# Folded output weights, packed attention output, full units for the last heads, and an ordered start in a two-block attention kernel

## The chip, the cores and the metric

The kernel runs on one core of one Trainium2 chip. The time is the device time of one execution in microseconds, from the first to the last instruction of the core with its start and end included. A kernel is run several times and the median is quoted. The trace of one execution gives a span that is some 2 us shorter than its time. An execution counts as slow, and is kept out of comparisons, when it lies more than 1.5% above the fastest one of the same kernel.

TensorE does the matmuls, VectorE and ScalarE the elementwise work and the copies out of PSUM, GpSimd small things, SyncE starts most transfers (its queue is SPq in the profile, that of ScalarE is ACTq).

## The reference

Two attention blocks of the same size work on separate inputs: 2,048 rows, width 640, 32 heads of 20. A is softmax attention, B is linear attention with the feature map phi.

```python
def _A_ref(x, wqkv, wo):
    q, k, v = split(x @ wqkv)                      # 32 heads of 20
    p = softmax(einsum("bhqd,bhkd->bhqk", q, k) * 20 ** -0.5)
    return merge(einsum("bhqk,bhkd->bhqd", p, v)) @ wo

def _B_ref(x, wqkv, wo):
    phi = lambda t: jnp.where(t > 0, t + 1, jnp.exp(t)) + 1e-6
    pq, pk = phi(q), phi(k)
    kv  = einsum("bhsd,bhse->bhde", pk, v)
    num = einsum("bhqd,bhde->bhqe", pq, kv)
    den = einsum("bhqd,bhd->bhq", pq, pk.sum(s))[..., None] + 1e-6
    return merge(num / den) @ wo

return concatenate([A, B], axis=-1)                # inputs times 0.05, bf16
```

## The kernel before

A's scores are small, so the exponential is replaced by its polynomial of second order: products of K's 20 columns (the features, on VectorE) are multiplied with V into a table f_Tu, and the same products of Q, taken unit by unit, are multiplied with that table. A unit is 512 rows of Q by 6 heads of 20 columns, 120 partitions. 32 heads make five such units and a short one of two heads.

```python
# first loads: x in two halves and K's weights whole, then V's weights
sch.dma("act", lambda e: e.dma_start(self.w[:, 1], awq[:, :, D_MODEL:2 * D_MODEL]), writes=(("w", 1),))
xnl(0)
sch.dma("sp", lambda e: e.dma_start(self.w[:, 2], awq[:, :, 2 * D_MODEL:3 * D_MODEL]), writes=(("w", 2),))
xnl(1)
# ... Q's columns are permuted on GpSimd:
sch.op("pool", lambda e, c=c: e.tensor_copy(
    self.w[:, 0, c, 0:600].rearrange("p (b a h) -> p b a h", b=5, h=6),
    self.w0r[:, c, 0:600].rearrange("p (b h a) -> p b a h", b=5, h=6)), ...)
# ... t_psi: a unit's Q rows come back from DRAM; the short unit (c == 5) needs six loads
if c < 5:
    fns = [lambda e: e.dma_start(sl[:, 0:4, :], self.q_load(c, qc, 0, 4, 1, True)),
           lambda e: e.dma_start(sl[:, 9:11, :], self.q_load(c, qc, 7, 2, 3, True))]
else:
    for x, (d, st, nj) in enumerate(((0, 0, 3), (0, 2, 3), (6, 2, 3), (1, 2, 3), (7, 2, 2))):
        fns.append(lambda e, ...: e.dma_start(self.slot[0:40 * nj, s, x, :], self.q_load(5, qc, d, nj, st, False)))
    fns.append(lambda e: e.dma_start(self.slot[80:120, s, 4, :], self.q_load(5, qc, 0, 1, 0, False)))
# ... t_norm, t_out: A's normalised output goes to DRAM (f_Od) and comes back in another layout
self.ost[G] = self.spd(fns, (m,), (("OTw", ow),), (("Od", G),), prio=0.6)
ol = self.spd([lambda e: e.dma_start(self.OTp[:, k], self.Od.ap()[:, col].rearrange("(c p) q -> p c q", p=128))], ...)
# ... B: numerator matmuls, then each of 20 results times the reciprocal of the denominator
sch.op("dve", lambda e: e.scalar_tensor_tensor(
    oT[:, c, :], ps[:, j.bank, :], self.cn[:, c:c + 1], self.Rb[:, k, :], op0=ALU.add, op1=ALU.mult), ...)
```

Cuts are marked by "...". The program does not write instructions in a fixed order. At build time a list scheduler simulates the engines with durations written in the code, and each time an engine is free takes the ready task of the lowest priority number. 21 of those numbers are constants that were fitted for this program:

```python
_C = dict(q=1.24, qs=0.0, ks=-0.005, kd=0.02, bk=1.83, bks=-0.005, bq=6.44, bo=0.03, out=0.46, pv=0.002,
          fe=1.73, psi=5.5, r=-1.04, f=0.92, nm=2.51, op=2.71, kv=1.87, npo=2.33, bqs=0.002,
          bd=-0.79, bn=3.42)
```

The order of every engine's instructions follows from them. Memory is reused, and the profile names it by its first user: f_xT also holds A's raw output, f_wB also B's reciprocals, f_Tu first the raw Q weights, f_pk first x.

## Time and profile before

| | before |
|---|---|
| time, median of 3 runs | 359.45 us (358.58 to 362.37) |
| span of the trace | 358.7 us |
| TensorE busy; mean granted clock | 303.6 us; 0.951 |
| of that, at full clock / lost to the clock | 290.3 / 13.3 us |
| TensorE idle | 55.1 us |
| moved by DMA | 58.85 MB |

The row "at full clock" is used throughout: the busy time of TensorE in each stretch of 5 us times the clock granted in that stretch, added up. It is what the same work would take with the clock never lowered. Full-clock work, clock loss and idle time add up to the span.

The prediction shows the main views. One stretch of the chain of waits of the kernel before is added here, because it became important afterwards (columns: start in us, us, engine or transfer with tile and line). It is a short unit on its way in:

```profile
181.35 0.91 SPq L1594
182.26 0.04 issue
182.31 0.69 SPq L1594
182.99 0.04 issue
183.03 2.31 SPq L1594
185.34 0.04 issue
185.38 7.86 DMA f_big<-f_Qd
193.24 0.02 issue
193.26 1.30 DVE f_big L1607 x2
```

The reader is to see that the engine at the top is the queue of SyncE: a load of a short unit holds it for 0.7 to 2.3 us before the next can start, and the fifth of the six loads lands 7.86 us after it was started. Only then does VectorE form the products. In shares of the span, that chain is

```profile
PE 53%; DMA 15%; DVE 11%; POOL 8%; SPq 6%; issue 5%; ACT 1%; ACTq 0%; DVEq 0%
```

so starting transfers took 6% of it, and GpSimd 8%.

### The profile page before, as it was taken

What the parts mean: (1) busy time and instruction counts of PE and PEld (TensorE: products, weight loads), DVE (VectorE), ACT (ScalarE), POOL (GpSimd) and SP (SyncE); (2) the same over time, 40 slices, a digit from 0 to 9 for tenths busy, and PEclk for the clock granted to TensorE, in tenths of its full rate; (3) what the DMA queues carried; (4) which work ended last, traced back from release to release, by engine and by line L of the source; (5) the groups of instructions that cost most, each with busy time, mean ns of one, the idle gap of its engine ahead of it and who ended that gap; (6) DMA issues with size and microseconds to landing.
All of it is one profiled execution on the core that took longest, in us unless ns stands there. A gap on an engine that the chain in (4) does not pass through costs nothing.

```text
span 358.7 us, 14998 instructions
## 1 busy us (share of the span) xinstructions
PE 303.6 (85%) x6834; PEld 198.4 (55%) x6834; DVE 253.3 (71%) x350; ACT 180.1 (50%) x377; POOL 31.3 (9%) x49
## 2 busy tenths in 40 slices
PE   5989579999998899879988299982999868789955
PEld 2657347777764356546744178741554324658723
DVE  2589699999988986878896349795658767441330
ACT  2775647888884235444433235442355535335413
POOL 0049880000020100000000000000000000000000
PEclk9999989999999699998999879998799989999988
DMA  7999548214247258277736947579874466566642
GB/s 264 250 212 136 90 92 248 57 49 126 59 132 201 62 133 246 65 190 201 191 119 178 203 119 256 146 166 242 227 206 140 133 185 213 164 228 199 210 141 82
DMA packets 63571, 58.85 MB, mean 164 GB/s; under 512 B 21036, under 2 KB 59980, under 8 KB 63500
## 3 DMA queue, kind: packets, MB, share of 16 engines
q1 hardware_dynamic: 58940, 49.99, 53.9%
q10 hardware_dynamic: 4560, 7.83, 7.3%
q8 instruction: 55, 0.90, 1.2%
q14 instruction: 16, 0.13, 0.1%
HBM read 39.65 MB, written 14.48 MB: 151 GB/s over the span
## 4 chain that ended last, share of the span: by engine, by line
PE 53%; DMA 15%; DVE 11%; POOL 8%; SPq 6%; issue 5%; ACT 1%; ACTq 0%; DVEq 0%
PE ps L172 52%; DMA f_big<-f_Qd 4%; SPq L1594 4%; DMA f_w<-f_Od 4%; POOL f_w L1157 3%; POOL f_st L1248 3%; DMA f_Rc<-f_xT 2%; DMA f_dc<-f_dn 2%; DMA f_pk<-in_A_x_dram 2%; DVE f_Tu L1449 2%; DMA f_wB<-f_Bd 1%; DVE f_pk L1993 1%; DVE f_big L1607 1%; DVE f_big L1357 1%; DVE f_big L1362 1%
## 5 line engine op out<-in xcount | busy, mean ns | idle before, releaser
L1607 DVE TENSOR_TENSOR f_big<-f_big 120x1536 bf16<-120x1536 bf16 (+2 forms) x68 | 67.6, 1001 | 8.4 <-DMA f_big<-f_Qd 7.0
L172 PE MATMUL ps<-f_wB,f_xB 128*32 128x320 bf16 x1280 | 52.2, 311 | 10.1 <-issue 8.0
L172 PE MATMUL ps<-f_big,f_Tu 120*32 120x512 bf16 (+2 forms) x880 | 53.4, 384 | 3.1 <-issue 1.7
L172 PEld LDWEIGHTS ps<-f_wB,f_xB 128*32 128x32 bf16 x1280 | 37.5, 100 | 21.7 <-issue 9.6
L172 PE MATMUL ps<-f_w,f_xT 128*32 128x320 bf16 x1280 | 48.4, 307 | 0.4 <-issue 0.2
L172 PEld LDWEIGHTS ps<-f_w,f_xT 128*32 128x32 bf16 x1280 | 34.3, 100 | 11.3 <-issue 0.8
L172 PEld LDWEIGHTS ps<-f_big,f_Tu 120*32 120x32 bf16 (+2 forms) x880 | 27.7, 98 | 23.2 <-issue 3.1
L1092 ACT COPY f_xT<-ps 126x512 f32<-126x512 f32 (+1 forms) x30 | 17.4, 587 | 39.2 <-PE ps L172 32.8
L172 PE MATMUL ps<-f_wo,f_w 128*32 128x320 bf16 x640 | 25.6, 320 | 6.9 <-DMA f_w<-f_Od 6.9
L1762 ACT ACTIVATE f_ex<-ps 128x320 f32<-128x320 f32 (+1 forms) x52 | 25.7, 498 | 11.3 <-PE ps L172 6.4
L1357 DVE TENSOR_TENSOR f_big<-f_big,f_Ks 128x3200 bf16<-128x3200 bf16 x16 | 30.3, 1896 | 1.3 <-ACT f_Ks L1092 1.3
L172 PE MATMUL ps<-f_xT,f_w 128*32 128x512 bf16 (+2 forms) x440 | 28.8, 408 | 2.6 <-POOL f_w L1160 2.5
L1092 ACT CAST f_st<-ps 128x320 bf16<-128x320 f32 x32 | 13.3, 426 | 34.5 <-PE ps L172 30.2
L172 PE MATMUL ps<-f_woB,f_pk 128*32 128x320 bf16 x640 | 25.1, 312 | 6.4 <-DVE f_pk L1993 5.9
L1362 DVE TENSOR_TENSOR f_big<-f_big 128x3200 bf16<-128x3200 bf16 x16 | 29.7, 1857 | 0.0
L172 PE MATMUL ps<-f_xB,f_wB 128*32 128x512 bf16 x400 | 28.8, 392 | 0.6 <-ACT f_ex L1762 0.6
L1993 DVE SCALAR_TENSOR_TENSOR f_pk<-ps,f_cn,f_wB 128x512 bf16<-128x512 f32 x20 | 14.0, 745 | 21.7 <-PE ps L172 18.4
L1758 DVE TENSOR_SCALAR f_r<-ps 128x320 f32<-128x320 f32 x32 | 14.8, 485 | 18.2 <-ACT f_ex L1762 17.0
L1092 ACT CAST f_pk<-ps 128x320 bf16<-128x320 f32 x32 | 13.5, 429 | 26.1 <-PE ps L172 25.6
L172 PEld LDWEIGHTS ps<-f_wo,f_w 128*32 128x32 bf16 x640 | 19.3, 103 | 12.9 <-DMA f_w<-f_Od 7.9
L172 PEld LDWEIGHTS ps<-f_woB,f_pk 128*32 128x32 bf16 x640 | 17.8, 101 | 13.5 <-DVE f_pk L1993 7.9
L1627 ACT ACTIVATE f_Dq<-f_big 120x512 bf16<-120x512 bf16 (+1 forms) x24 | 15.1, 628 | 13.2 <-DMA f_big<-f_Qd 11.3
(125 smaller groups left out, 386.4 us busy)
## 6 DMA issues: line engine op xcount, KB each, us to landing
f_big<-f_Qd SPq DMA_DIRECT2D x20, 480.0 KB, 8.0
f_Qd<-f_OTw SPq DMA_DIRECT2D x40, 120.0 KB, 2.5
f_big<-f_Qd SPq DMA_DIRECT2D x20, 240.0 KB, 8.8
f_w<-f_Nd ACTq DMA_DIRECT2D x4, 720.0 KB
f_Rbc<-f_Nd ACTq DMA_DIRECT2D x4, 720.0 KB
f_wB<-f_Bd SPq DMA_DIRECT2D x12, 240.0 KB
f_w<-f_Od SPq DMA_DIRECT2D x4, 640.0 KB
out_dram<-f_st SPq DMA_DIRECT2D x16, 160.0 KB, 3.3
```

The source lines that it names most:

```text
L172: lambda e: e.matmul(out, lhsT, rhs, start=start, stop=stop, tile_position=tp, skip_group_check=sgc),
L1092: return self.sch.op("act", lambda e: e.copy(out, in_), reads=reads, writes=writes)
L1157: sch.op("pool", lambda e, c=c: e.tensor_copy(self.w[:, 0, c, 0:600].rearrange("p (b a h) -> p b a h", b=5, h=6), self.w0r[:, c, 0:600].re ...
L1248: ops.append((lambda e, x=x, a=a, n=n, b=b: e.tensor_copy(self.P[:, x, 6 * a:6 * (a + n)].rearrange("p (a h) -> p a h", h=6), self.ident[0 ...
L1357: sch.op("dve", lambda e: e.tensor_tensor(F[:, :, 122:222].rearrange("p h (d a) -> p h d a", a=20), k0.unsqueeze(2).broadcast_to([128, 32, ...
L1362: sch.op("dve", lambda e: e.tensor_tensor(F[:, :, 22:122].rearrange("p h (d a) -> p h d a", a=20), k0.unsqueeze(2).broadcast_to([128, 32, ...
L1594: fns.append(lambda e, x=x, d=d, st=st, nj=nj: e.dma_start(self.slot[0:40 * nj, s, x, :], self.q_load(5, qc, d, nj, st, False)))
L1607: return e.tensor_tensor(x[:, o:o + n, :], x[:, a:a + 1, :].broadcast_to([p, n, 512]), x[:, b:b + n, :], op=ALU.mult)
L1627: sch.op("act", lambda e: e.activation(self.Dq[0:120 if c < 5 else 40, dq, :], src, AF.Square), reads=(k0,), writes=(("Dq", dq),))
L1758: sch.op("dve", lambda e: e.tensor_scalar(r1, ps[:, j.bank, 0:n], 0.0, 1e-6, op0=ALU.max, op1=ALU.add), reads=(("ps", j.bank),), writes=(( ...
L1762: sch.op("act", lambda e: e.activation(ex, ps[:, j.bank, 0:n], AF.Exp), reads=(("ps", j.bank),), writes=(("ex", k, h),))
L1993: sch.op("dve", lambda e: e.scalar_tensor_tensor(oT[:, c, :], ps[:, j.bank, :], self.cn[:, c:c + 1], self.Rb[:, k, :], op0=ALU.add, op1=AL ...
```

## The change

The intent: (1) B's kv matrix is multiplied into B's output weights once (the fold), so that the numerator matmuls and their 20 products go, and the reciprocal is put on the features of Q in four long products; (2) A's output is packed by units of 120 rows, in the layout in which it is needed, so that the trip through DRAM goes; (3) the last two heads of all 2,048 rows are regrouped into one full unit of 512 columns and one of 176, with two loads each; (4) the first loads come in half tiles in a strict order, the constants are made in the first 10 us, mostly on VectorE, and the permutation of Q's weights moves to ScalarE, with a second one for B; (5) the priorities were fitted anew. The core of the diff:

```diff
-_C = dict(q=1.24, qs=0.0, ks=-0.005, kd=0.02, bk=1.83, bks=-0.005, bq=6.44, ...
+_C = dict(q=0.62, qs=0.04, ks=0.0, kd=0.02, bk=1.68, bks=0.0, bq=-2.52, ...
 # first loads
-        sch.dma("act", ... self.w[:, 1], awq[:, :, D_MODEL:2 * D_MODEL] ...)
-        xnl(0)
-        sch.dma("sp", ... self.w[:, 2] ...)
-        xnl(1)
+        xnl(0, 0, "sp")
+        for h in range(2):
+            sch.dma("act", ... self.w[:, 1, :, 320 * h:320 * h + 320] ...)
+        xnl(0, 1, "act")
+        sch.dma("act", ... self.w[:, 2] ...)
+        sch.barrier(("sp",), (("w", 1, 1),))
+        xnl(1, 0, "sp")
+        xnl(1, 1, "sp")
 # permutation of Q's weights
-        self.ew[0] = plan.add(_Task("pool", 6.0, perm, prio=0.5), (e0,))
+        self.ew[0] = plan.add(_Task("none", 0.0, lambda t: None), [plan.add(_Task(
+            "act", 0.9, lambda x, c=c: perm(x, c), prio=1.0), (e0,)) for c in range(N_DC)])
+        self.ewB[0] = plan.add(_Task("none", 0.0, lambda t: None), [plan.add(_Task(
+            "act", 0.75, lambda x, c=c: permB(x, c), prio=2.2), (e1,)) for c in range(N_DC)])
 # constants
-        last = self.event(14.0)
+        last = self.event(1.5)
 # units: every unit has two loads, the last heads are units "S0" (512 columns) and "S1" (176)
-            for x, (d, st, nj) in enumerate(((0, 0, 3), (0, 2, 3), (6, 2, 3), (1, 2, 3), (7, 2, 2))):
-                fns.append(lambda e, x=x, d=d, st=st, nj=nj: e.dma_start(...))
-            fns.append(lambda e: e.dma_start(self.slot[80:120, s, 4, :], self.q_load(5, qc, 0, 1, 0, False)))
+        fns = [lambda e: e.dma_start(sl[:, 0:4, :], self.q_load(u, 0, 4, 1)),
+               lambda e: e.dma_start(sl[:, 9:11, :], self.q_load(u, 7, 2, 3))]
 # A's output: straight into the packed tile
-        self.ost[G] = self.spd(fns, (m,), (("OTw", ow),), (("Od", G),), prio=0.6)
+                sch.op("dve", lambda e: e.tensor_tensor(self.OTw[0:120, kw, c:c + nu, :], self.OTr[0:120, r:r + nu],
+                                                        self.Rbc[rb][0:120, 0:nu], op=ALU.mult), ...)
 # B: kv times the output weights once, through DRAM into the wanted row order
+                        self.fm(ps[:, b, 0:320], self.KVT[:, c, 128 * k:128 * (k + 1)], self.woB[:, c2, hc], ...)
+        m1 = self.spd([lambda e: e.dma_start(md.rearrange("(c p) n -> p c n", p=128), self.Mn)], mps, ...)
+        mld = self.spd([lambda e, i=i: e.dma_start(self.Mp[32 * i:32 * i + 32], ...) for i in range(4)], (m1, bar), ...)
 # B: one product of 2,560 elements for each 512 rows in place of five numerators and five products
-                    oT[:, c, :], ps[:, j.bank, :], self.cn[:, c:c + 1], self.Rb[:, k, :], op0=ALU.add, op1=ALU.mult), ...)
+                    pqT, pqT, 1e-6, self.Rb[:, k, :].unsqueeze(1).broadcast_to([128, N_DC, 512]), op0=ALU.add, op1=ALU.mult), ...)
```

Not shown: buffers, the selection of table columns for the last heads, some transfer times written into the plan (for A's reciprocal 4.0, 4.0 and 6.5 us before, 6.0, 4.8 and 8.0 after), and VectorE's order of the first features (the ten repeated columns of K are copied first, so that the even products need not wait for the odd ones).

## The prediction

> **What bounds the kernel now.** I read the page's busy shares first, then the slices, then the windows, then what TensorE waited for, then the chain that ended last, then the groups of instructions. Busy shares and slices (tenths of each fortieth of the span, some 9 us a slice):
>
> ```profile
> span 358.7 us, 14998 instructions
> PE 303.6 (85%) x6834; PEld 198.4 (55%) x6834; DVE 253.3 (71%) x350; ACT 180.1 (50%) x377; POOL 31.3 (9%) x49
> ...
> PE   5989579999998899879988299982999868789955
> ...
> PEclk9999989999999699998999879998799989999988
> ```
>
> TensorE is the bound on average, with 358.7 - 303.6 = 55.1 us in which it does nothing. The reader should see where the row is not 9: the first slices, slice 5, slices 23 and 28, and the last ten. The windows (length, then busy us of PE, PEld, DVE, ACT, POOL with counts, granted clock, DMA share, GB/s) put sizes on it:
>
> ```profile
> 0.00:10.00 10.00, 6.13 (x36) 3.32 (x40) 3.03 (x11) 2.84 (x5) 0.86 (x7) 1.00 0.83 275
> 40.00:60.00 20.00, 13.43 (x344) 9.62 (x348) 19.33 (x15) 10.36 (x25) 12.70 (x8) 0.91 0.60 136
> 60.00:80.00 20.00, 20.00 (x580) 14.94 (x574) 19.77 (x19) 17.45 (x39) 0.27 (x1) 1.00 0.28 82
> ...
> 200.00:220.00 20.00, 13.74 (x308) 10.88 (x311) 9.64 (x15) 6.70 (x16) 0.00 (x0) 0.83 0.71 172
> 240.00:260.00 20.00, 13.40 (x283) 7.46 (x279) 13.47 (x22) 7.78 (x16) 0.00 (x0) 0.83 0.94 237
> ```
>
> Two regimes. Up to about 105 us VectorE paces: at 40 to 100 us it is busy over 95%, and per row tile its three feature instructions cost 1.90 + 1.86 + 0.81 = 4.56 us, 73 us for 16 tiles, while TensorE uses the spare time for B's projections. After that TensorE paces, with holes. What TensorE waited for (total, times, longest):
>
> ```profile
> PE ps L172 <- issue: 10.0, 6, 6.7
> PE ps L172 <- DMA f_w<-f_Od: 6.9, 2, 6.5
> PE ps L172 <- DVE f_pk L1993: 6.7, 7, 2.3
> PE ps L172 <- DVE f_big L1362: 4.8, 3, 4.4
> PE ps L172 <- DVE f_xB L1781: 4.8, 2, 3.4
> ...
> PE ps L1283 <- DMA f_pk<-in_A_x_dram: 2.9, 1, 2.9
> PE ps L172 <- POOL f_w L1160: 2.5, 1, 2.5
> ```
>
> Five of these seven belong to things that the change removes or moves: f_Od (A's output bounced through DRAM), L1993 (B's numerator times reciprocal), the first load, GpSimd's permutation of A's Q weights, and indirectly the 4.4 us on L1362. The 6.7 us of "issue", at 199.60, have no cause in the profile. The chain (start, us, what) shows the two largest clearly:
>
> ```profile
> 1.27 6.36 DMA f_pk<-in_A_x_dram
> ...
> 39.85 2.50 POOL f_w L1157
> ...
> 236.94 13.48 DMA f_w<-f_Od
> ```
>
> GpSimd makes its selection constants from 23.3 to 38.4, then permutes f_w until 52.5, and TensorE starts Q only then.
>
> **What the Trainium skill says.** (1) "TensorE: Matmul & The Clock Gate", Part 1: TensorE's clock falls back to half after an idle window of about 3.4 us. The trace agrees: the two windows with gaps of 6.66 and 6.52 us have a granted clock of 0.83, against 1.00 in their neighbours, so a removed gap is worth more than its length. (2) "DMA: Bandwidth & Descriptors", Anatomy of one DMA: a transfer has a fixed cost of about 2 us, most of it the write receipt. Here it is more under load: 36 KB to f_Rc took 7.43 us and 64 KB to f_dc 6.85 us on the chain. A removed round trip through DRAM is thus worth two such latencies, whatever its bytes. (3) "VectorE: DVE Perf Modes", the TRN2 errata: an fp32 tensor_tensor of N elements takes (N+151)/0.96 ns, 691 ns at 512. The related instruction of L1781 took 665 to 688 ns at 512 and 811 at 640, so the fit serves.
>
> **The change part by part.**
>
> TensorE. B's numerator matmuls go: rows f_xB,f_kvN 5.2 + f_pq,f_kvN 3.2 + f_Vp,f_kvN 2.5 = 10.9 us. In their place the block-diagonal kv is multiplied into B's output weights once: 10 steps of 128 columns (about 0.07 us each, 0.7 us) and 26 steps of 320. The f_woB row does 160 such steps in 25.1 us, 0.157 each, so 4.1 us. Selection of table columns for the last heads adds about 0.5 and the small constants lose 0.4. The last heads: before 4 units of 4 steps of 512 columns, after one full unit of 12 steps of 512 and one of 12 steps of 176: 8,192 against 8,256 columns, nothing. Net -10.9 + 0.7 + 4.1 + 0.5 - 0.4 = -6.0 us, nearly 1:1 in the TensorE-paced half.
>
> VectorE. Away: 20 numerator products (14.0 us); the products of 4 short units, 4 x (0.96 + 0.41) = 5.5; the A products fall from 14.0 to about 12.7 as pairs take 1,024 elements; other small ones 3: 23.8. New: 4 products over 2,560 elements at (2560+151)/0.96 = 2.82 us, 11.3; the full unit 1.21 + 2 x 0.96 = 3.1 and the narrow one about 1.45, from the slope of 0.5 ns an element between those rows; table spreads 2.3; fold 1: 19.2. Net -4.6 us. Some 6 us of constants move into the first 10 us, where VectorE is busy 3.03.
>
> ScalarE takes GpSimd's permutation, five at about 0.9 us, and a second one for B, five at 0.74, plus some 6 us of fold copies. It loses 16 x 0.22 us as two copies to f_Ks become one of 896 elements. About +7 us on an engine at 50%: hidden.
>
> DMA and the queues. A's output round trip goes (2.6 MB each way); B's reciprocal broadcast falls from 5.1 MB in 52 issues to 1.0 MB in 16 and loses one of its three hops; loads and stores of features fall by 2.8 MB; the fold adds 1.6. About 11 MB of 58.85 in all. SyncE issues some 45 fewer, at about 0.7 us each 31 us of its queue. In particular six loads per short unit, which stand on the chain three times with about 5.5 us each (4% of the span on L1594), become two.
>
> Path, in us. TensorE work -6.0. First loads in order: 320 KB of x and 400 KB of weights at 275 GB/s are 2.6 us, so the first projection, at 9.71 before, should start near 6.3, and VectorE's first feature near 11 instead of 14.34: -3.4, kept, as VectorE paces. Constants and permutation off GpSimd: 2.5 + half of 4.4, less what it trades: -3.5. The f_Od gap 6.5 plus 1.5 of cold clock (my estimate: half a window), of which another wait takes some: -5. Waits on L1781 and L1993, 4.8 + 6.0 after 280 us: half, -5. Late feature loads: -1.5. The unexplained "issue" gap: -1, as it may recur. New waits of the fold (kv to transposed copy to product to DRAM and back, two hops of 6 to 7 us) and of the last normalisation: +3. Sum -22.4, so 359.45 - 22.4 = 337.
>
> **The rivals.** (a) The end becomes A's: B's output now ranks before A's, so after the last scores the chain store, reciprocal, store, broadcast, product, output stands with little left to fill it. Three hops of 5 to 8 us each: TensorE would idle up to 15 us at the end, giving about 350. Against it: the priorities were retuned, so B's output should be the filler; the old end lost 8 us too. (b) GpSimd's constants are planned at 9 us but took 15.1; VectorE's in-order queue then stands at the masks that need GpSimd's counters, in its paced phase: up to 5 us, 342. For it: VectorE did wait 3.4 us on them once. Against: seven of the copies are gone. (c) Transfers and idle were hidden anyway and VectorE stays the bound in the first 105 us: then only the start and the TensorE work count, -9, 350. (d) All holes close but start, table stage and end (about 25 us): 297 + 25 = 322.
>
> **Range and chances.** Rivals (a) and (c) set the upper end, 350; (d) with some rest the lower, 325. Predicted 337 us, 325 to 350 in 8 of 10. Faster by over 2% means under 352.3, which needs only -7: TensorE's work and the start give that alone, so 0.90. Within 2% 0.08; slower 0.02, if the fold or the masks stall an engine for tens of us.
>
> **What would show it.** TensorE busy near 297, mean clock above 0.951; first projection near 6.3 and first feature near 11 us; no f_Od anywhere, Q not released by GpSimd; DMA near 48 MB; four long products of about 2.8 us at B's normalisation; last table work 6 to 9 us earlier than 120. Wrong if TensorE's idle time stays near 55 us, merely moved to the end or to the fold, or if VectorE waits on GpSimd in the first 30 us.

## The result

| | before | after |
|---|---|---|
| time, median | 359.01 us (4 runs) | 329.37 us (4 runs: 326.26 to 331.02) |
| ratio of fast runs | | 0.9181, interval 0.9078 to 0.9285 |
| span of the trace | 358.7 us | 324.1 us |
| TensorE work at full clock | 290.3 us | 282.4 us |
| lost to the clock | 13.3 us | 7.5 us |
| TensorE idle | 55.1 us | 34.2 us |
| moved by DMA | 58.85 MB | 47.60 MB |

A ratio is the mean time of one kernel's fast runs over that of the other's of the same rounds, so it is not quite the ratio of the medians beside it. Worked back from the runs, this one leaves the profiled run of each kernel out; with all fast runs it is 0.9156. The four runs before are the three quoted above and one of 356.97 us beside the runs of the changed kernel, all fast.

The two profiled spans differ by 34.6 us, a little more than the medians (29.6), as the profiled run was the fastest of its four. Of the 34.6, 7.9 are less work, 5.8 less clock loss and 20.9 less idle time. The page of the kernel after, the lines that answer to those of before:

```profile
span 324.1 us, 14979 instructions
PE 289.9 (89%) x6866; PEld 203.3 (63%) x6866; DVE 249.9 (77%) x341; ACT 190.8 (59%) x390; POOL 10.0 (3%) x35
...
PE   6888959997999989998997969997988997999995
PEclk9799999999999978999799997999999999999999
...
PE 60%; DVE 14%; ACT 11%; DMA 7%; issue 5%; ACTq 1%; SPq 1%; POOL 0%; POOLq 0%; DVEq 0%
```

Slices are 8.1 us here and were 9.0 before. No slice is at 2 any more, where two were, and of the last ten only the very last is under 7. The hole in the table stage is still there, though smaller, now in slice 6 (41 to 49 us): the permutation of Q's weights, on ScalarE from 39.42 to 46.65, stands where GpSimd's stood. TensorE waits 2.33 and 1.02 us there, where it waited 4.38 and 2.50 before. In the chain, transfers fell from 15 to 7%, GpSimd from 8 to 0 and the starting of transfers from 6 to 1; ScalarE rose from 1 to 11. The windows say the same with sizes (columns as in the prediction):

```profile
0.00:10.00 10.00, 6.00 (x46) 2.74 (x50) 6.57 (x29) 2.80 (x7) 3.66 (x19) 0.91 0.85 276
...
40.00:60.00 20.00, 16.12 (x396) 9.84 (x392) 12.89 (x14) 17.05 (x31) 0.00 (x0) 1.00 0.70 165
60.00:80.00 20.00, 17.94 (x562) 15.29 (x554) 19.62 (x17) 16.85 (x33) 0.00 (x0) 1.00 0.46 122
...
200.00:220.00 20.00, 20.00 (x465) 12.29 (x458) 19.15 (x33) 10.64 (x22) 1.70 (x1) 1.00 0.58 143
...
240.00:260.00 20.00, 17.11 (x321) 8.33 (x313) 16.12 (x21) 10.99 (x20) 0.00 (x0) 1.00 0.94 238
```

The two windows that held a gap of 6.5 us now have the clock at 1.00 in place of 0.83, and 6.3 and 3.7 us more of TensorE. But the first 10 us have no more TensorE work than before, and up to 120 us both kernels had done nearly the same: 102.6 us of full-clock work before, 103.5 after. So all of the gain lies after the table. What TensorE waited for:

```profile
PE ps L172 <- issue: 9.6, 8, 2.4
PE ps L172 <- DVE f_big L1364: 3.1, 2, 2.3
PE ps L172 <- DVE f_xT L1095: 3.0, 1, 3.0
PE ps L172 <- ACT f_pk L1091: 2.9, 3, 2.1
```

No single wait is over 3.0 us; before, three were over 4. The start explains why the first window gained nothing (timeline of the kernel after, TensorE; start, duration, and in brackets the idle time and who ended it):

```profile
4.37 1.17 PE L1287 MATMUL ps<-f_id,f_pk 128*128 128x128 bf16 x10
5.53 0.59 PE L172 MATMUL ps<-f_w,f_xT 128*32 128x320 bf16 x12
9.11 3.74 PE L172 MATMUL ps<-f_w,f_xT 128*32 128x320 bf16 x68 [2.99 <-DVE f_xT L1095]
```

The first projection begins at 5.53 instead of 9.71, does 12 matmuls and then stands until 9.11, for a transposed half tile whose copy sits on VectorE behind the constants that the change put there (VectorE's timeline, the last four rows up to that copy):

```profile
7.20 0.76 DVE L1247 MEMSET f_kva<- 128x840 f32 x1
8.00 0.41 DVE L1248 MEMSET f_dn<- 128x420 uint32 x1
8.45 0.46 DVE L1249 MEMSET f_kvN<- 128x480 uint32 x1
8.83 0.23 DVE L1095 COPY f_xT<-ps 128x256 bf16<-128x256 bf16 x1
```

The table at 110 us, one line of VectorE's timeline before and one after:

```profile
113.21 10.90 DVE L1449 TENSOR_TENSOR f_Tu<-ps,f_M 123x504 bf16<-123x504 f32 x16
```

```profile
112.89 14.01 DVE L1456 TENSOR_TENSOR f_Tu<-ps,f_M 123x504 bf16<-123x504 f32 x24 [0.57 <-PE ps L172]
```

(A row takes in pieces of several sizes and is named by one.) It begins at the same time and has 24 pieces in place of 16, so it ends at 126.9. Before, the 16 pieces ended at 124.1, and six small ones for the short unit followed until 125.4. So the whole table is done 1.5 us later than before.

### The profile page after: what moved, and what is told of

Same layout as the page of the kernel before. It is cut to its first block, busy times and chain, and to the rows that moved or that the text cites. A ratio compares the mean times of both kernels' runs of the same rounds, so it can differ in the third digit from the quotient of the medians.

```text
span 324.1 us, 14979 instructions
## 1 busy us (share of the span) xinstructions
PE 289.9 (89%) x6866; PEld 203.3 (63%) x6866; DVE 249.9 (77%) x341; ACT 190.8 (59%) x390; POOL 10.0 (3%) x35
## 2 busy tenths in 40 slices
DMA packets 59413, 47.60 MB, mean 147 GB/s; under 512 B 23645, under 2 KB 58265, under 8 KB 59345
## 4 chain that ended last, share of the span: by engine, by line
PE 60%; DVE 14%; ACT 11%; DMA 7%; issue 5%; ACTq 1%; SPq 1%; POOL 0%; POOLq 0%; DVEq 0%
PE ps L172 60%; DMA f_Rc<-f_xT 3%; DVE f_big L1369 2%; DVE f_big L1364 2%; ACT f_w L1091 2%; DMA f_Nd<-f_Rc 2%; DMA f_big<-f_Qd 2%; ACT f_big L1091 2%; DVE f_Tu L1456 1%; ACT f_qk L1091 1%; ACT f_wB L1091 1%; ACT f_big L1345 1%; ACT f_Ks L1091 1%; DVE f_big L1601 1%; SPq L1589 1%
## 5 line engine op out<-in xcount | busy, mean ns | idle before, releaser
L1601 DVE TENSOR_TENSOR f_big<-f_big 120x1536 bf16<-120x1536 bf16 (+3 forms) x66 | 67.0, 1016 | 4.2 <-DMA f_big<-f_Qd 2.7
L172 PE MATMUL ps<-f_big,f_Tu 120*32 120x512 bf16 (+4 forms) x968 | 57.4, 373 | 6.0 <-issue 4.5
L172 PE MATMUL ps<-f_wB,f_xB 128*32 128x320 bf16 x1280 | 53.4, 309 | 2.5 <-issue 2.5
L172 PEld LDWEIGHTS ps<-f_wB,f_xB 128*32 128x32 bf16 x1280 | 42.5, 100 | 8.8 <-issue 3.3
L172 PEld LDWEIGHTS ps<-f_big,f_Tu 120*32 120x32 bf16 (+2 forms) x968 | 31.5, 97 | 24.8 <-issue 6.2
L172 PEld LDWEIGHTS ps<-f_w,f_xT 128*32 128x32 bf16 x1280 | 34.8, 99 | 15.3 <-DVE f_xT L1095 3.2
L1091 ACT COPY f_xT<-ps 126x512 f32<-126x512 f32 (+3 forms) x33 | 16.8, 530 | 38.1 <-PE ps L172 35.0
L1776 ACT ACTIVATE f_ex<-ps 128x320 f32<-128x320 f32 (+1 forms) x52 | 25.5, 500 | 16.5 <-PE ps L172 13.3
L1091 ACT CAST f_pk<-ps 128x320 bf16<-128x320 f32 (+3 forms) x64 | 25.5, 417 | 15.8 <-PE ps L172 12.7
L172 PE MATMUL ps<-f_xT,f_w 128*32 128x512 bf16 (+2 forms) x440 | 27.2, 395 | 1.6 <-ACT f_w L1091 1.0
L1772 DVE TENSOR_SCALAR f_r<-ps 128x320 f32<-128x320 f32 x32 | 15.2, 486 | 12.5 <-ACT f_ex L1776 10.5
L172 PE MATMUL ps<-f_xB,f_wB 128*32 128x512 bf16 x400 | 23.9, 379 | 0.3 <-ACT f_ex L1776 0.3
L1614 ACT ACTIVATE f_Dq<-f_big 120x512 bf16<-120x512 bf16 (+1 forms) x22 | 13.6, 619 | 13.7 <-DMA f_big<-f_Qd 11.2
L1091 ACT CAST f_qk<-ps 120x512 bf16<-120x512 f32 (+1 forms) x24 | 13.5, 586 | 12.0 <-PE ps L172 11.9
L172 PEld LDWEIGHTS ps<-f_xT,f_w 128*32 128x32 bf16 (+2 forms) x440 | 11.3, 98 | 14.5 <-ACT f_w L1091 2.0
L1091 ACT CAST f_big<-ps 128x320 bf16<-128x320 f32 (+1 forms) x33 | 14.3, 442 | 9.7 <-PE ps L172 9.3
L172 PE MATMUL ps<-f_big,f_Vp 128*32 128x242 bf16 x512 | 16.3, 267 | 3.5 <-DVE f_big L1364 3.1
```

The source lines that it names most:

```text
L172: lambda e: e.matmul(out, lhsT, rhs, start=start, stop=stop, tile_position=tp, skip_group_check=sgc),
L1091: return self.sch.op("act", lambda e: e.copy(out, in_), reads=reads, writes=writes)
L1601: sch.op("dve", lambda e: e.tensor_tensor(sl[:, o:o + n, :], sl[:, a:a + 1, :].broadcast_to([120, n, N]), sl[:, b:b + n, :], op=ALU.mult), ...
L1614: sch.op("act", lambda e: e.activation(self.Dq[0:120, dq, 0:N], sl[:, 0, :], AF.Square), reads=(k0,), writes=(("Dq", dq),))
L1772: sch.op("dve", lambda e: e.tensor_scalar(r1, ps[:, j.bank, 0:n], 0.0, 1e-6, op0=ALU.max, op1=ALU.add), reads=(("ps", j.bank),), writes=(( ...
L1776: sch.op("act", lambda e: e.activation(ex, ps[:, j.bank, 0:n], AF.Exp), reads=(("ps", j.bank),), writes=(("ex", k, h),))
```

## The experiments

All kernels gave correct results. Each is compared with the kernel before in the same rounds on the same chip. The fast runs of the kernel before had medians of 359.01, 356.83, 357.84 and 356.31 us in the four sets of rounds, so kernels of different rounds are compared by their ratio to it, and differences are given in per cent of before. The changed kernel itself was run in the first set only. In the second and the fourth set some runs of the kernel before were slow and are left out (2 of 7 and 5 of 11).

| kernel | fast runs | their median, us | ratio to before | interval |
|---|---|---|---|---|
| after | 4 of 4 | 329.37 | 0.9181 | 0.9078 to 0.9285 |
| e1: before with the fold | 1 of 4 | 355.42 | 1.0160, see there | 1.0083 to 1.0238 |
| e2: after, no fold | 2 of 4 | 336.55 | 0.943 | none |
| e3: after, trip through DRAM | 4 of 4 | 338.54 | 0.9503 | 0.9419 to 0.9588 |
| e4: after, old start | 4 of 4 | 333.47 | 0.9365 | 0.9297 to 0.9434 |
| e5: before, after's priorities | 4 of 4 | 364.45 | 1.0215 | 1.0150 to 1.0281 |
| e6: before with the fold, after's priorities | 3 of 4 | 371.45 | 1.0447 | 1.0362 to 1.0531 |
| e7: after, before's priorities | 2 of 4 | 339.14 | 0.948 | none |
| e8: after, B's permutation on GpSimd | 4 of 4 | 325.99 | 0.9148 | 0.9069 to 0.9226 |
| e9: before, searched | 4 of 4 | 348.69 | 0.9785 | 0.9713 to 0.9858 |
| e10: before with the fold, searched | 3 of 4 | 349.73 | 0.9823 | 0.9734 to 0.9912 |
| e11: after, trip through DRAM, searched | 4 of 4 | 326.38 | 0.9141 | 0.9081 to 0.9202 |
| e12: the version of part 5 | 5 of 6 | 317.61 | 0.8905 | 0.8846 to 0.8963 |

The two ratios without an interval are worked out here as the mean of all fast runs over that of before in those rounds. Worked back from the runs, the others leave the profiled runs out in the first three sets (after and e1 to e8) and count them in the last (e9 to e12). With the profiled fast runs counted everywhere, after has 0.916, e3 0.949, e4 0.936, e5 1.019, e6 1.038 and e8 0.914, which changes no reading below.

### 1. Parts alone and parts undone

The fold alone in the kernel before, old priorities, B's permutation with it:

```diff
+        self.KVT = self.pkf[:, 0:1920].rearrange("p (c n) -> p c n", c=N_DC)
+                    self.fm(ps[:, b, 0:320], self.KVT[:, c, 128 * k:128 * (k + 1)], self.woB[:, c2, hc], ...
-        (the numerator matmuls and their 20 products)
```

> The kernel before with only B's fold put in (its own priorities, its own A, its own start). If the fold's terms of the prediction hold (TensorE work -10.9 + 4.8, half of the 10.8 us of waits on B's normalisation, +3 for the fold's own two hops), it is 7 to 9 us faster than before, near 351 us, with TensorE busy near 298. If instead the gain comes from the new order of work as a whole (the retuned priorities), the fold alone under the old priorities gives less than 3 us or costs something, because its hops land where nothing fills them.

Measured: one run of 355.42 us, which is the profiled one, and three of 361.68 to 365.03, which are slow by the rule since they lie over 1.5% above the first. The work fell as worked out, 284.3 us at full clock against 290.3, the 6.0 of the prediction, with idle time as before (55.8 against 55.1). But the one fast run is hardly faster than before's own fast runs of these rounds (355.90 to 357.92), and the ratio of 1.0160 is made of the three slow runs. No gain can be seen, but a run like this does not settle it; e10 below does better.

The changed kernel without the fold (old numerators, reciprocal hops and output weights; one staging buffer had to move):

```diff
-                    pqT, pqT, 1e-6, self.Rb[:, k, :].unsqueeze(1)...      (four products)
+                    oT[:, c, :], ps[:, j.bank, :], self.cn[:, c:c + 1], self.Rb[:, k, :], ...  (twenty)
```

> The changed kernel with B's numerators, three-hop reciprocal and output weights as before, everything else of the change kept. Fold theory: 7 to 12 us slower than the changed kernel, 336 to 341, TensorE busy back up by about 6. Order theory: within 3 us of the changed kernel's 329, as the planner finds other work for the holes.

Measured: fast runs of 336.68 and 336.41 us, two more slow ones, a ratio of 0.943: 2.5% of before more than the changed kernel. Taken out of the changed kernel the fold seems worth some 9 us; put into the old one it gives nothing. Both cannot be its price. The changed kernel without the fold was not searched anew, so what the fold is worth there stays open.

The changed kernel with A's output through DRAM again, by groups, in the packed layout:

```diff
-                sch.op("dve", lambda e: e.tensor_tensor(self.OTw[0:120, kw, c:c + nu, :], ...
+                sch.op("dve", lambda e: e.tensor_tensor(self.bst[0:120, k, 0:nu, :], ...
+            b1 = self.spd([lambda e: e.dma_start(od, self.bst[0:120, k, 0:nu, :]...)], (m,), ...)
+                sch.dma_group("sp", [lambda e: e.dma_start(self.OTw[0:120, kw, c:c + nu, :]..., od)], ...)
```

> The changed kernel with A's normalised output again written to DRAM and read back before the output matmuls (360 or 240 KB each way per group), still packed. If the removed round trip was worth its 6.5 us gap, it is 4 to 8 us slower, 333 to 337, the most of it after the last group, where little is left to fill. If round trips are hidden by filler in the new order, it is within 2 us of 329.

Measured: 338.54 us, ratio 0.9503, 3.2% of before more than the changed kernel. That looks like a confirmation of the f_Od term, and more. Part 4 takes it back.

The changed kernel with the old first loads, and with the constants starting at 14 us in the plan:

```diff
-        xnl(0, 0, "sp")           (half tiles in strict order)
+        sch.dma("act", ... self.w[:, 1] ...)    (the old five lines)
-        last = self.event(1.5)
+        last = self.event(14.0)
```

> The changed kernel with the loads of the kernel before (whole tiles side by side) and the constants begun at 14 us again. The prediction gave the start 3.4 us and the constants part of 3.5: then it is 4 to 7 us slower, 333 to 336. The trace after shows the table stage beginning at 112.9 us against 113.2 before, so my theory now is that VectorE's and ScalarE's queue in the first 100 us ate the gain: then it is at most 2 us slower.

Measured: 333.47 us, ratio 0.9365, 1.8% of before more than the changed kernel (4.1 us between the two medians), and the intervals do not touch. My theory after reading the traces, that the start gave at most 2 us, fell. But the prediction's path does not hold either. VectorE's first feature, in its timeline:

```profile
12.16 1.83 DVE L1365 TENSOR_TENSOR f_big<-f_big 128x3200 bf16<-128x3200 bf16 x1 [2.91 <-ACT f_big L1091]
```

It comes at 12.16 with the old start and at 12.17 with the new one, and at 14.34 in the kernel before. So the 2 us there come from the other order of the first copies and products, not from the loads. In the trace 4.1 us more are idle and 2.9 more lost to the clock, and one wait of 4.95 us (for ScalarE, until 44.16) stands where the changed kernel has the 2.33 and 1.02 of above. Which of the edits that comes from, or whether it is again a poorer order, stays open.

### 2. The order by itself

The next runs change no work at all, only the 21 priorities. First the kernel before, and the kernel with the fold, with the changed kernel's priorities:

```diff
-_C = dict(q=1.24, qs=0.0, ks=-0.005, kd=0.02, bk=1.83, ...      (before's)
+_C = dict(q=0.62, qs=0.04, ks=0.0, kd=0.02, bk=1.68, ...        (after's)
```

> The kernel before with nothing but the 21 priorities of the changed kernel. If the gain is largely the new order, it is several us faster than before (under 350). My theory is that the priorities only pay together with the parts that they were tuned for: then it is within 2% of 358 or slower.

Measured: 364.45 us, ratio 1.0215: slower by 2%.

> The fold on the kernel before, which gave nothing under the old priorities (361.7, TensorE busy 6 us less, idle 6 us more), now under the new ones. If the saved work turned into idle time because the old order put the fold and its four chains where nothing fills them, the new priorities bring 5 to 12 us: 346 to 353. If the fold needs the packed A output and the early start as well, it stays at 355 to 362.

Measured: 371.45 us, ratio 1.0447. My theory that the fold's gain was only waiting for the new priorities fell.

Then the changed kernel with the old priorities (the same two lines exchanged):

> The changed kernel under the old priorities. If order and parts go together it loses 8 us or more: 337 to 350. If the parts carry the gain whatever the order, it is within 4 us of 329.

Measured: fast runs of 341.25 and 337.02 us, and two slow ones just over the limit (342.73 and 342.74); a ratio of 0.948, 3.0% of before more than with its own priorities (2.5 without the profiled runs, 3.3 with them in both). Its idle time is 45.0 us against 34.2 and its clock loss 11.2 against 7.5; the full-clock work is the same within 1 us.

Priorities thus belong to one program: each set is worse on the other's, by 2 to 3%. It is tempting to read the single removals as a bill: 2.5% for the fold, 3.2 for the trip, 1.8 for the start and 3.0 for the priorities. But they add up to 10.5%, while the whole change is 8.2, and the full units are not even in the bill. The items overlap, since each removal also spoils the fitted order. Undoing a part measures the part and the misfit together.

### 3. Is ScalarE the pace of the middle?

In the changed kernel ScalarE is busy 19.52 of 20 us at 80 to 100 us, and B's permutation is part of it. It was moved to GpSimd, which has nothing to do then:

```diff
-            "act", 0.75, lambda x, c=c: permB(x, c), prio=2.2), (e1,)) for c in range(N_DC)])
+            "pool", 2.7, lambda x, c=c: permB(x, c), prio=2.2), (e1,)) for c in range(N_DC)])
```

> The changed kernel with B's weight permutation (five copies of 1.42 us on ScalarE, planned at 0.75) on GpSimd, which is busy 3%. ScalarE is busy 19.52 of 20 us at 80 to 100 us. If it sets the pace there, this wins 3 to 6 us (323 to 326); if the features on VectorE or the order do, it is within 2 us of 329.

Measured: 325.99 us, ratio 0.9148, within the interval of the changed kernel. The time lies in the range expected if ScalarE paced, but the kernel before was faster in these rounds too, and the ratios differ by 0.3% of before. So no gain is shown: ScalarE was not what paced, or what it paced was made good elsewhere.

### 4. Parts compared after each program got its own order

So each hybrid got priorities of its own: some 5,300 to 6,600 sets were tried against the program's own plan (its simulated end, not a time of the chip), and the best was run. First the kernel before, with nothing else changed:

```diff
-_C = dict(q=1.24, qs=0.0, ks=-0.005, ..., fe=1.73, psi=5.5, r=-1.04, f=0.92, ...
+_C = {'q': 2.56, 'qs': 0, 'ks': 0.079, ..., 'fe': 2.0, 'psi': 3.29, 'r': 0.14, 'f': -1.2, ...
```

> The kernel before, nothing changed but its 21 priorities, which I searched anew against the program's own plan (5,286 trials, the best of three searches). It tells how much of the 29.6 us any search of the order would have given without a single part. If order alone explains the gain: under 345. If the parts are needed: 350 or more.

Measured: 348.69 us, ratio 0.9785. Some 2% lay in the order of the old kernel alone. Its waits of TensorE, two rows of the list:

```profile
PE ps L172 <- issue: 8.5, 6, 2.8
...
PE ps L172 <- DVE f_pk L1991: 3.1, 3, 2.1
```

No row with f_Od is left in that list, though the trip through DRAM is all there, the long "issue" gap is gone, and the wait for B's products (line 1991 here, 1993 before) fell from 6.7 to 3.1 us. Of three holes that the prediction counted as gain, two closed and one halved by order alone, for 2% of the time. Others opened: TensorE now waits up to 5.7 us for ScalarE (f_Dq), and the loss to the clock is 12.9 us, hardly less than the 13.3 before.

The kernel before with the fold, searched in the same way:

> The fold on the kernel before, searched in the same way (5,764 trials). Under the old and under the changed kernel's priorities the fold lost time (361.7 and 371.8 us). If only its order was at fault, it now beats the searched kernel before by the 6 us of TensorE work and more: 6 to 12 us faster than that one. If the fold needs the other parts, it is no faster than that one.

Measured: 349.73 us, ratio 0.9823, where the same kernel without the fold has 0.9785; its profile fell into a slow run (354.02 us) and is not used for sizes. Fitted or not, no gain of the fold alone shows in the old kernel. (A search against the plan finds a good order, not surely the best on the chip.)

The changed kernel with A's output through DRAM, searched:

> The changed kernel with A's output bounced through DRAM, searched in the same way. Unsearched it took 338.5, 9 us more than the changed kernel. If the bounce itself costs that (its latency after the last group, 5 MB more traffic), it stays 5 us or more above 329. If 338.5 came from an order made for another program, it comes to within 3 us of 329.

Measured: 326.38 us, ratio 0.9141, no slower than the changed kernel's 0.9181, with 52.54 MB moved in place of 47.60. The same kernel with the changed kernel's priorities (e3) had 0.9503, so that loss went with a new order. The time of the changed kernel is reached with this trip, by groups and in the packed layout, as well; but the changed kernel's own order was not searched in this way, so the comparison is not quite even. What the removal gives on top of a searched order was not run by itself; part 5, which has three more edits, lies 2.4% lower.

Between the last two, both searched, both with the fold and with the trip, lie 6.8% of before (0.9823 and 0.9141), 23 us between their fast medians. What still differs between them: the last heads as full units, A's packed layout, the start with its constants, the permutation, the order of the first copies, and some transfer times in the plan. The shares of the chain of waits, first of the searched kernel before (e9), then of the searched changed kernel with the trip (e11):

```profile
PE 33%; DMA 25%; DVE 22%; SPq 8%; POOL 5%; issue 3%; ACT 2%; ACTq 1%; DVEq 0%
```

```profile
PE 68%; ACT 10%; DVE 10%; DMA 7%; issue 4%; ACTq 0%; SPq 0%; POOL 0%; POOLq 0%
```

A better order alone did not take the queue of SyncE and the transfers off the old kernel's chain; they grew, from 6 and 15% to 8 and 25%. In the kernel with full units they are at 0 and 7%, although it moves only 6.3 MB less. But not all of the 8% belongs to short units: by line they have 3% (L1592), and 4% are loads of B's reciprocals (L1970), which the fold thins out from 52 to 16. In the searched kernel with the fold and the short units (e10; a slow run, so only as a pointer) the short units' loads alone have 8% of the chain. Nor is a share a measure of time: the fastest kernel of all (part 5) has 15% of transfers on its chain.

SyncE's own timeline shows what was in that queue (start, us, queue, line, operation, tiles, count). First the loads of a short unit in the kernel before and what came after them, then those of a full unit in the kernel after:

```profile
227.22 5.38 SPq L1594 DMA_DIRECT2D f_big<-f_Qd  x5
232.65 1.67 SPq L1596 DMA_DIRECT2D f_big<-f_Qd  x1
234.49 1.82 SPq L1589 DMA_DIRECT2D f_big<-f_Qd  x1
236.35 0.49 SPq L1590 DMA_DIRECT2D f_big<-f_Qd  x1
236.94 0.40 SPq L1717 DMA_DIRECT2D f_w<-f_Od  x1
```

```profile
215.71 0.32 SPq L1589 DMA_DIRECT2D f_big<-f_Qd  x1
216.07 0.49 SPq L1590 DMA_DIRECT2D f_big<-f_Qd  x1
```

Six loads hold the queue for 7.0 us, two for 0.8. The last row of the first block is the load of A's output for which TensorE stood the 6.52 us until 250.47: on the chain it comes straight after these eight feature loads, which had held the queue since 227.22. So the gap that the prediction charged to the trip was in part a queue in front of it.

Summed over such rows, feature loads took 61.2 us of SyncE's queue before (27.2 of them for four short units), 53.4 in the searched kernel before, 24.8 after, and 26.7 in the searched kernel with the trip. The loads of B's reciprocals fell too, from 37.8 us of the queue before and 38.1 in the searched kernel before to 11.3 after. The median from issue to landing of the two kinds of loads of full units fell from 8.0 and 8.8 us to 5.1 and 6.1 (5.6 and 9.0, and 5.2 and 6.9, in the two searched kernels).

This makes the full units the first candidate for what remains of the 6.8% after the start, but it is argued, not shown, and the other differences listed above, the plan's transfer times among them, were not tested by themselves: a run with the changed kernel and the old short units, with an order of its own, would show it, and was not made, since it needs table, layouts and grouping rewritten.

### 5. A version that beats both

Three things that the traces had shown were mended in the changed kernel: B's permutation on GpSimd, A's permutation planned at the time it takes (1.45 us a step), and three clears of B's tables moved from VectorE's first constants to GpSimd; then the priorities were searched.

```diff
-            "act", 0.9, lambda x, c=c: perm(x, c), prio=1.0), (e0,)) for c in range(N_DC)])
+            "act", 1.45, lambda x, c=c: perm(x, c), prio=1.0), (e0,)) for c in range(N_DC)])
-            "act", 0.75, lambda x, c=c: permB(x, c), prio=2.2), (e1,)) for c in range(N_DC)])
+            "pool", 2.7, lambda x, c=c: permB(x, c), prio=2.2), (e1,)) for c in range(N_DC)])
+        for o in ((lambda e: e.memset(self.kvacc[:], 0.0), (), ("kva0",)), ...mask, ...kvN):
+            task("pool", 1.2, o)
-_C = dict(q=0.62, qs=0.04, ...
+_C = {'q': 0.89, 'qs': 0.024, ...
```

> A version meant to beat both: the changed kernel with B's weight permutation on GpSimd, the three clears of B's tables taken out of VectorE's early queue (they held the fifth transposed copy, so that TensorE stood 3.0 us at 6 to 9 us), A's permutation planned at its measured 1.45 us a piece, and the priorities searched for this program (6,631 trials). Expected 318 to 326; if it stays at 326 to 330, the plan no longer sees what limits the kernel.

Measured: 317.61 us, ratio 0.8905, 3% under the changed kernel's ratio, and the intervals do not touch. The start in its timeline of TensorE, to be held against 9.11 and 2.99 above:

```profile
7.46 2.49 PE L172 MATMUL ps<-f_w,f_xT 128*32 128x320 bf16 x68 [1.08 <-DVE f_xT L1096]
```

The wait for the half tile fell to 1.08 us, the first feature came at 9.60, idle time fell to 29.4 us and the clock loss to 5.7. How the 3% divide between these edits and the search is not known.

All sums of the profiled fast runs, by the method given above:

| kernel | span | at full clock | lost to clock | idle |
|---|---|---|---|---|
| before | 358.7 | 290.3 | 13.3 | 55.1 |
| before, searched | 347.7 | 287.8 | 12.9 | 46.9 |
| before with the fold | 353.6 | 284.3 | 13.5 | 55.8 |
| after, no fold | 334.9 | 286.3 | 8.1 | 40.5 |
| after, trip through DRAM | 335.2 | 281.8 | 10.9 | 42.5 |
| after, trip, searched | 324.7 | 280.9 | 8.9 | 34.8 |
| after, old start | 330.7 | 282.1 | 10.4 | 38.3 |
| after, old priorities | 339.4 | 283.2 | 11.2 | 45.0 |
| after | 324.1 | 282.4 | 7.5 | 34.2 |
| the version of part 5 | 316.8 | 281.6 | 5.7 | 29.4 |

Work differs by some 10 us in all of them, idle time and clock loss by 33. This kernel's time is decided by how well its waits are filled. (Full-clock work of one and the same set of matmuls differs by up to 2.5 us between orders, as the pairs before and before searched show, since some records are missing and ends are modelled.)

## Why the prediction was right or wrong

The time lies in the range, 7.6 us below the predicted 337, and the direction and most signs were right. The steps of the sum were not.

- **TensorE's work, -6.0: right in size.** The fold alone gave 290.3 - 284.3 = 6.0; the whole change 7.9. Busy time was put "near 297" and was 289.9, since clock loss fell too. **What it is worth is not borne out**: "nearly 1:1 in the TensorE-paced half" failed in the old kernel, where the fold alone, searched or not, gave no gain that the runs can tell from nothing.
- **The start, -3.4, and the constants and permutation, -3.5: wrong path.** The projection started at 5.53, earlier than the predicted 6.3, and then stood for 2.99 us behind the very constants that the prediction had put on VectorE as harmless ("where VectorE is busy 3.03"). The first feature came at 12.17, not 11. The table work was to end 6 to 9 us earlier than 120: it ended at 126.9 (the kernel before had ended it at 125.4, not at 120). Q's projection did come 8 us earlier (44.33 in place of 52.54), but the table gained nothing from it. By 120 us TensorE was ahead by 0.9 us of work, against some 7 predicted. Undoing the start still costs 1.8% of before, by a way that no run shows.
- **The f_Od gap, -5: the wait went, its removal was not needed.** Both long gaps and their low clock are gone (0.83 to 1.00 in both windows). But the gap closes with the trip in place too: in the old kernel by a search alone, and in the changed kernel with the trip put back and searched no wait for f_Od is left either, and the time is no longer than the changed kernel's (0.9141 and 0.9181). In the trace before, the load stood behind eight feature loads in SyncE's queue (part 4) and then took 13.48 us to land: the gap was at least in part one of order and queue, not the price of the trip alone.
- **Waits on L1781 and L1993, -5.** They are gone, but in the old kernel a search alone halves the larger one and removes the other, and the fold that was to remove them gives nothing there, so the term is not shown as a cause.
- **Late feature loads, -1.5: mis-sized.** The prediction had counted the issues rightly (some 45 fewer; the timelines list 259 and 212) and had the six loads of a short unit on the chain, 4% of the span on L1594 alone, some 15 us. It then gave them 1.5. The whole share of SyncE's queue on the chain went from 6 to 1%, and that of transfers from 15 to 7. How much of the 6.8% between the two searched kernels is theirs is open.
- **The "issue" gap, -1.** The total stayed (10.0 and 9.6 us), but the long gap did not come back (longest 6.7 and 2.4), nor in the searched kernel before (2.8).
- **The clock, +1.5 within the f_Od term: too small.** It gave 5.8 us. The mechanism was right, and the trace agrees with the Trainium skill ("TensorE: Matmul & The Clock Gate", Part 1) on the low clock after a long gap: with the two gaps of over 6 us gone, their windows went from 0.83 to 1.00, which is 4.6 of the 5.8 us (27.1 us busy in them, times 0.17).
- **New waits, +3.** Near. Of the fold, TensorE waits 0.9 us for a long product and 1.3 us for denominators (f_dn); no wait for the round trip of the folded weights is among its waits.
- **Left out: the order.** The priorities were in the diff and the prediction used them only as an argument against rival (a). The old kernel gains 2.1% from a search alone, the changed one loses some 3% of before with the old set. Whether the changed kernel's set is a better fit of its program than the old one was of its own is not known: a fresh search on the changed kernel with nothing else edited was not run.

The four products took 2.75 to 2.82 us (2.82 predicted). The group of two of them in the kernel after (busy us, then mean ns, then VectorE's idle time before them):

```profile
L2028 DVE SCALAR_TENSOR_TENSOR f_xB<-f_xB,f_wB 128x2560 bf16<-128x2560 bf16 x2 | 5.6, 2824 | 2.4 <-DMA f_wB<-f_dc 2.4
```

DMA fell to 47.60 MB (48 predicted), the mean clock rose from 0.951 to 0.974, f_Od is gone. VectorE did not stand on GpSimd's constants, so rival (b) did not come. Rival (a), an empty end, did not come either: TensorE is busy 19.48 of the last full 20 us. Rival (c) was half right: before 120 us nothing was gained, but after it far more than the work. The mechanism is nearest to rival (d), which left start, table stage and end as they were and filled the waits between; its 322 took idle time as 25 us, and it was 34.2.

That the total came out near is in part chance: the sum gave 16 us to the fold's saved work, its waits and the f_Od gap (6, 5 and 5). Of these the fold shows no gain in the old kernel, and the time is reached without removing the trip. It gave almost nothing to the queue, the clock and the order.

## What to carry to other kernels

In a program whose instruction order is fitted, taking a part out measures the part together with the misfit; fit the order of each variant anew before giving the part a price. Here that turned the loss of 3.2% for one part into none that shows. Count how many transfers a unit of work starts on one queue, not only their bytes, since six small loads can hold it for 7 us, as here, and what stands behind them waits. And look at what is put ahead of a short critical copy on the same engine: here constants and clears came back as a hole of 2.99 us, and in the best version, with three clears moved away, it was 1.08. Writing measured durations into the plan was part of the best version, but what it alone gave is not known.

## What the Trainium skill lacked or had wrong

- "ScalarE: Activation LUTs", What ACT_TABLE_LOAD costs, gives 186 ns + 0.833 ns an element for an ACTIVATE with immediate scale and bias. That fits ScalarE's copy of 896 elements in K's feature tile (933 ns by the formula, 940 measured). It does not fit the permuting copies within a partition: 640 elements took 1,416 ns and 600 took 1,264, where the formula gives 719 and 686. The group of B's permutation in the kernel after (busy us, mean ns, idle before):

```profile
L1091 ACT COPY f_wB<-f_Tu 128x640 bf16<-128x640 bf16 x5 | 6.9, 1416 | 0.0
```

  These copies read with a step of 20 elements and took 1.8 to 2.0 times the formula; no page that I found gives a time for that. The step alone need not be the reason: the copies of 40 elements, with the same step but only two heads, took 224 ns (219 by the formula). The program's plan (0.75 and 0.9 us) and the prediction were off by it. GpSimd takes 2,406 (600 elements, before) and 2,639 to 2,698 ns (640, in e12 and e8) for the same copies.
- "DMA: Bandwidth & Descriptors", Anatomy of one DMA, gives about 2 us plus the bytes over 436 GB/s, fitted on transfers from GpSimd. Feature loads of 480 KB from SyncE took 8.0 us in the median before and 5.1 after (3.1 by that fit, my estimate), so 4.9 and 2.0 us more, with other transfers in flight. The page has no such figure for loads from SyncE beside others.
- No page that I found gives, for this chip, how long starting one such load holds the issuing queue. Here a load of a full unit held it for 0.85 us on average before (4.99 at most, at 196.41) and 0.52 after, and one of a short unit for 1.13.
